# A fused attention and feed-forward kernel: the second product's seven-product form with four products in one bank, copies by ScalarE or VectorE, squares in place

## The chip, the cores and the metric

One core of one Trainium2 chip runs the whole program. Its engines are TensorE (PE, with PEld for its weight loads), VectorE (DVE), ScalarE (ACT), GpSimd (POOL) and SyncE (SP); each works through its own list of instructions in order and waits on semaphores for the others. POOL and SP also start DMA transfers. The metric is the device time of one execution in microseconds; a change is judged by the median of several runs.

## The reference

Eight batches of eight heads, 576 positions, 64 wide. Heads 0 to 3 see the last 32 positions, heads 4 to 7 every 32nd one. The attention's output, as a matrix x of 4608 tokens by 512, goes through a feed-forward layer with a squared ReLU:

```python
def _attn_ref(q, k, v):
    scores = scale * np.matmul(q, k.transpose(0, 1, 3, 2))
    scores = np.where(masks[None, :, :, :], scores, -1000000000.0)
    attn = softmax(scores)
    return np.matmul(attn, v)

def _moe_ref(x, w_in, w_out, s, b):
    h = x @ w_in                  # 4608 x 512 by 512 x 2048
    r = np.maximum(h, 0.0)
    g = s * (r * r) + b
    return g @ w_out              # 4608 x 2048 by 2048 x 512
```

Since b is one number, g @ w_out is s times (r*r) @ w_out plus b times the column sums of w_out. The kernel keeps those sums, times b, in the tile `bcs`.

## The kernel before

The attention runs over 8 batches and, in each, over 4 pairs of heads (two local pairs, two strided ones). For one pair: transposes of q and k (TensorE or DMA), scores (L656), exp on ScalarE (L674), a mask product on VectorE (L682), the product with v (L717, into banks `t` and `a`), a reciprocal (L734) and a scaling into `x_nat` (L744) on VectorE, and a transposition into `xT`. The scaling frees the bank for the next product with v.

The feed-forward layer runs over nine blocks T = 0 to 8 of 512 tokens. The first product (L1016, for T = 7 and 8 a seven-product form, L1241) gives 16 tiles h of 128 by 512; ScalarE writes relu(h) to a buffer u (L1042), and two tiles at a time are squared into `gT` by VectorE (L1052) or ScalarE (L1050). The second product takes `gT` and `w_out`: in a plain form for T = 0 and 1 (L1271), and for T = 2 to 8 in a form with seven half-size products P1 to P7 in place of eight (`ff2_seven`, L984), 16 matmuls of 256 columns each. For it, VectorE makes four sums S of parts of `gT` (L852) and once four sums of parts of `w_out` (`w_mix`, L878). The results, four quarters C11, C12, C21, C22 of a block's output, come together in PSUM and in tiles in SBUF:

- Va = s X + b from P1; then P2 goes on top of P1 in the same bank, and C11 = s X + b.
- Ua = s Y + Va from P6; Ub = Ua + (b2 - b1), the difference of the two halves of `bcs`; Vb = s Z + Ub from P7.
- C22 = s W + Vb from P5, then P3 on top of it: C12 = s W + Ub. P4 goes on top of P7: C21 = s Z + Ua.

Va, Ua, Vb (L903) and the four stores (L915) are scalar-tensor-tensor instructions of VectorE, 0.75 us each; the Ub adds (L926) are VectorE's but for one that GpSimd does.

GpSimd starts the loads of each batch (`fetch_qk`, `fetch_v`): q and k, then v, up to eighteen DMAs, behind two small copies (`gate`, L1356) that wait for the transposes of an earlier batch's k. SyncE starts the transposing DMAs and the output's.

The order of everything is fixed when the program is built. `Plan` keeps an estimate of the time of each engine; TensorE's steps come in the order of lists (attention `att`, first product `f1`, second product `f2`) as their inputs become ready by that estimate, and the work of the other engines is posted with a cost for each engine that may do it and taken up by the time it becomes ready, plus a number from the table `ORDER` for its kind and for one of four stretches of time. Where a posted job names two engines, the one that would end first gets it. PSUM has eight banks: t, a, s0, s1, f10, f11 (first product) and f20, f21 (second).

Of the kernel before, what the change touches and what calls it, by code (L numbers as in the profile page):

```python
# [1637 lines left out]
```

## Time and profile before

| | before |
|---|---|
| median of 3 runs | 297.75 us (297.03, 297.75, 298.77) |
| span of the profiled execution | 295.5 us (its own whole time is not on the page) |
| GpSimd busy | 92.8 us, 31% |
| VectorE busy | 236.8 us, 80% |
| ScalarE busy | 194.6 us, 66% |
| DMA traffic | 38.19 MB, 129 GB/s in the mean |

The page is one execution. "Busy" counts an engine's instructions, the chain follows the instruction that ended last back to what released each step, and groups put together the instructions of one source line. Starts are in us from the span's start. A row of the timeline merges instructions of one kind that follow each other: its length runs from the first start to the last end. Matmuls overlap, so their spacing is read from starts, not from lengths.

### The profile page before, as it was taken

The numbers are of one execution on the slowest core, as the hardware profiler recorded it, in microseconds if no ns is written. First come the engines' busy times: TensorE is split into PE (matmuls) and PEld (weight loads), VectorE is DVE, ScalarE is ACT, GpSimd is POOL, SyncE is SP. The second block draws the span as 40 slices with busy tenths as digits, with TensorE's granted clock in tenths as the row PEclk, the third lists the DMA queues.
The fourth block names the chain that finished last, engine by engine and source line by source line (L and its number), as shares of the span: only waits on it lengthen the run. The fifth ranks groups of instructions, "written<-read, shape, count | busy, mean of one in ns | idle before, by whom it ended". The sixth has DMA issues, their size and how long they took to land.

```text
span 295.5 us, 7106 instructions
## 1 busy us (share of the span) xinstructions
PE 289.5 (98%) x2803; PEld 219.3 (74%) x2803; DVE 236.8 (80%) x498; ACT 194.6 (66%) x334; POOL 92.8 (31%) x140
## 2 busy tenths in 40 slices
PE   7899999999999999999999999999999999999995
PEld 3775655665565567989867785779888999999984
DVE  5765977888976789768986888688899689888874
ACT  3667855897967797947873777478966564576500
POOL 8872623610961396008820195200002000000000
PEclk9999999999999999999999999999999999999999
DMA  8999999999999699979999999998430300210314
GB/s 131 180 206 203 213 184 174 208 189 128 140 160 145 98 91 161 160 138 146 162 149 147 169 168 130 134 137 213 44 104 13 109 35 2 71 38 0 109 39 143
DMA packets 106152, 38.19 MB, mean 129 GB/s; under 512 B 85414, under 2 KB 103974, under 8 KB 106118
## 3 DMA queue, kind: packets, MB, share of 16 engines
q0 software_dynamic: 60848, 18.23, 64.2%
q1 hardware_dynamic: 45270, 19.51, 36.1%
q8 instruction: 22, 0.36, 0.5%
q14 instruction: 12, 0.10, 0.1%
HBM read 36.99 MB, written 10.62 MB: 161 GB/s over the span
## 4 chain that ended last, share of the span: by engine, by line
PE 95%; POOL 3%; DVE 1%; issue 1%; ACT 0%; POOLq 0%
PE ps_f L1016 32%; PE ps_f L984 25%; PE ps_f L1271 8%; PE ps_s L656 5%; PE ps_f L1241 3%; PE ps_a L717 3%; PE ps_t L1241 2%; PE ps_s L984 2%; PE ps_a L1241 2%; PE ps_s L1241 2%; PE ps_t L717 1%; PE ps_t L984 1%; PE ps_s L1271 1%; PE ps_f L717 1%; PE ps_t L535 1%; PE ps_f L535 1%
## 5 line engine op out<-in xcount | busy, mean ns | idle before, releaser
L1016 PE MATMUL ps_f<-xT,w_in_sb 128*128 128x512 f16 (+4 forms) x568 | 115.3, 331 | 0.0
L1042 ACT ACTIVATE u<-ps_f 128x512 f16<-128x512 f32 x107 | 62.8, 595 | 34.5 <-PE ps_f L1016 32.4
L1016 PEld LDWEIGHTS <-w_in_sb 128*128 128x128 f16 x576 | 57.1, 114 | 23.1
L984 PEld LDWEIGHTS <-gT 128*128 128x128 f16 x608 | 58.3, 98 | 8.6
L984 PE MATMUL ps_f<-w_out_sb,gT 128*128 128x256 f16 x376 | 53.4, 273 | 0.0
L1271 PE MATMUL ps_f<-w_out_sb,gT 128*128 128x512 f16 x112 | 31.9, 379 | 0.0
L674 ACT ACTIVATE p_str<-ps_s 72x432 f16<-72x432 f32 (+1 forms) x45 | 21.1, 488 | 10.1 <-PE ps_s L656 9.5
L1052 DVE TENSOR_TENSOR gT<-u 128x1024 f16<-128x1024 f16 x32 | 21.8, 682 | 5.2 <-ACT u L1042 4.8
L1050 ACT ACTIVATE gT<-u 128x1024 f16<-128x1024 f16 x24 | 25.4, 1058 | 0.7
L984 PE MATMUL ps_f<-w_mix,gT 128*128 128x256 f16 x176 | 24.9, 273 | 0.0
L674 ACT ACTIVATE p_loc<-ps_s 128x384 f16<-128x384 f32 x46 | 20.7, 489 | 5.5 <-PE ps_s L656 5.1
L744 DVE TENSOR_TENSOR x_nat<-ps_a,rec 72x384 f16<-72x384 f32 (+2 forms) x45 | 23.5, 523 | 0.7
L852 DVE TENSOR_TENSOR gT<-gT 128x1024 f16<-128x1024 f16 x34 | 22.4, 683 | 0.3 <-ACT gT L1050 0.3
L415 POOL DMA_DIRECT2D v_loc<-in_v_dram x24 | 17.8, 767 | 10.1 <-DMA w_out_sb<-in_moe_w_out_dram 4.2
L984 PEld LDWEIGHTS <-S 128*128 128x128 f16 x176 | 17.1, 98 | 2.7
L717 PEld LDWEIGHTS <-p_str 72*128 72x128 f16 x256 | 13.6, 98 | 5.8 <-ACT p_str L674 0.7
L420 POOL DMA_DIRECT2D v_str<-in_v_dram x16 | 13.0, 817 | 12.8 <-PE ps_f L1016 3.7
L1271 PEld LDWEIGHTS <-gT 128*128 128x128 f16 x128 | 11.4, 98 | 6.9 <-issue 0.2
L1356 POOL COPY gate<-kT 1x1 f16<-1x1 f16 x6 | 2.2, 371 | 45.0 <-DMA kT<-ks 45.0
L984 PE MATMUL ps_f<-w_mix,S 128*128 128x256 f16 x112 | 15.0, 273 | 0.0
L734 DVE RECIPROCAL rec<-ps_a 72x6 f32<-72x6 f32 (+2 forms) x45 | 8.3, 184 | 8.4 <-PE ps_a L717 8.0
L717 PEld LDWEIGHTS <-p_loc 128*128 128x128 f16 x192 | 11.2, 98 | 5.0 <-ACT kTs L437 0.8
(235 smaller groups left out, 543.1 us busy)
## 6 DMA issues: line engine op xcount, KB each, us to landing
out_dram<-o SPq DMA_DIRECT2D x34, 256.0 KB
w_in_sb<-in_moe_w_in_dram POOLq DMA_DIRECT2D x4, 512.0 KB, 9.9
w_out_sb<-in_moe_w_out_dram POOLq DMA_DIRECT2D x4, 512.0 KB, 10.7
qs<-in_q_dram POOLq DMA_DIRECT2D x6, 288.0 KB, 8.1
ks<-in_k_dram POOLq DMA_DIRECT2D x6, 288.0 KB, 9.9
v_loc<-in_v_dram POOLq DMA_DIRECT2D x24, 72.0 KB, 9.8
ql<-in_q_dram POOLq DMA_DIRECT2D x4, 288.0 KB, 9.9
kl<-in_k_dram POOLq DMA_DIRECT2D x16, 72.0 KB, 3.7
```

Of the source, the lines that this page charges most:

```text
L415: nc.gpsimd.dma_start(out=vl[LPAD:128, h, :, 0:D], in_=v_band(b, h))
L674: nc.scalar.activation(out=st["pw", g][0:nk, 0:2 * n * nq], in_=st["s", g][0:nk, 0:2 * n * nq], func=AF.Exp, scale=scale)
L717: nc.tensor.matmul(out=st["pa", g][:, n % 6, :], lhsT=st["pw", gp_][0:nk, i * nq:i * nq + WIDE], rhs=vt[0:nk, 2 * mm + e, j, :])
L744: nc.vector.tensor_tensor(out=x_at(0, cnt), in0=st["pa", g][0:nq, 0:cnt, 0:D], in1=st["rec", g][0:nq, 0:cnt].to_broadcast([nq, cnt, D]), o ...
L852: {"V": nc.vector, "P": nc.gpsimd}[eng].tensor_tensor(out=at(out), in0=at(x), in1=at(y), op=op)
L984: nc.tensor.matmul(out=gts[name, T, t][:, 0] if halves else gts[name, T][:, t], lhsT=lhs(k, t), rhs=rhs(k), start=fresh and k == 0 and (ha ...
L1016: nc.tensor.matmul(out=gts["h", T, ft][:, lo:hi], lhsT=w_in_sb[ft // 4][:, ct].rearrange("p (x l) -> p l x", l=4)[:, ft % 4], rhs=xT[ct][: ...
L1042: nc.scalar.activation(out=u, in_=gts["h", T, ft], func=AF.Relu)
L1050: nc.scalar.activation(out=g, in_=u, func=AF.Square)
L1052: nc.vector.tensor_tensor(out=g, in0=u, in1=u, op=ALU.mult)
L1241: nc.tensor.matmul(out=st[bk][:, 256 * t:256 * t + 256], lhsT=lhs(t, c), rhs=rhs(c), start=fresh and t == c == 0, stop=t == c == 1, skip_g ...
L1271: nc.tensor.matmul(out=gts[id_], lhsT=gts[T][:, ft, ts * 128:(ts + 1) * 128], rhs=w_out_sb[:, ft, cols], start=(ft == 0), stop=(ft == NFT ...
```

## The change

It does four things.

1. For T = 2 to 7, `ff2_chain` takes the place of `ff2_seven`. P1, P6, P5 and P3 add up in one bank (A); P2 has a bank of its own (C), P7 and P4 share another (D). After P1, P6 and P5 the sum so far is kept in SBUF as s A + b: V (tile `cp_v`), U (`cp_u`) and E (again `cp_v`). Each of these three copies is either one instruction of VectorE, or a scaled copy on ScalarE followed by an add of b on GpSimd. The next product that goes into A waits for the copy alone. C11 = s C + V, C22 = s D + E, C12 = s A + b, C21 = s D + U are stored by VectorE. Block 8 keeps `ff2_seven`, with its tiles in other places.
2. relu(h) is written to `gT` and squared in place; the buffers u and their waits are gone.
3. In the seven-product form of the first product the sums go to `gT` too, and wait for the second product of block T - 2 as a whole.
4. Every number of `ORDER` is drawn anew.

Of the 18 copies, 14 go by ScalarE and GpSimd: V at T = 2, 3, 5, 6; U at T = 2 to 7; E at T = 2, 4, 6, 7. Four are VectorE's.

```diff
 ORDER = [
-    {"g": 0.0, "S": -2500.0, "in": 500.0, "w_mix": 2500.0, "wc": 0.0, "ev": 2500.0, "c21": -200.0,
+    {"g": 200.0, "S": 2500.0, "in": 500.0, "w_mix": 200.0, "wc": -200.0, "ev": 200.0,
...
+    def ff2_chain(T):
...
+        def combine(out, of, plus):
+            nc.vector.scalar_tensor_tensor(out=out, in0=gts[of, T], scalar=s_sb[:, 0:1],
+                                           in1=plus, op0=ALU.mult, op1=ALU.add)
+
+        def keep(name, half, then):
+            def add(eng):
+                nc.gpsimd.tensor_tensor(out=own_tile(name), in0=own_tile(name), in1=b[half],
+                                        op=ALU.add)
+
+            def g(eng):
+                if eng == "V":
+                    combine(own_tile(name), "A", b[half])
+                    return [d(then)]
+                nc.scalar.activation(out=own_tile(name), in_=gts["A", T], func=AF.Copy,
+                                     scale=s_sb[:, 0:1])
+                plan.post([d(then + "s")], {"P": 1700.0}, add, [d(then)])
+            return g
...
+        EV = {"V": 750.0}
+        KEEP = {"V": 750.0, "A": 700.0}
...
+            ("P1", A, "A", True, cut(0, 0), w(0, 0), gn(0), [("bcs",)],
+             [([d("P1")] + ([("c11", T - 1)] if T > SEVEN else []), KEEP,
+               keep("V", 0, "Va"), [d("Vas")])]),
+            ("P2", C, "C", True, cut(0, 1), w(1, 0), gn(1), [],
+             [([d("P2"), d("Va")], EV, store(0, 0, "C", lambda: own_tile("V")),
+               [d("c00"), C])]),
+            ("P6", A, "A", False, tile_of("S2") if roomy(T) else cut(0, 0), mix(2), sn(2),
+             [("w_mix", 2), d("Vas")],
+             [([d("P6")] + prior, KEEP, keep("U", 0, "Ua"), [d("Uas")])]),
+            ("P7", Dd, "D", True, tile_of("S"), mix(3), sn(3), [("w_mix", 3)], []),
+            ("P5", A, "A", False, cut(1, 0), mix(1), sn(1), [("w_mix", 1), d("Uas")],
+             [([d("P5"), d("c00")], KEEP, keep("V", 1, "Ea"), [d("Eas")]),
+              ([d("P7"), d("Ea")], EV, store(1, 1, "D", lambda: own_tile("V")), [d("c11")])]),
+            ("P3", A, "A", False, tile_of("S4") if roomy(T) else cut(0, 1), w(1, 1), sn(4),
+             [d("Eas")], [([d("P3")], EV, store(0, 1, "A", lambda: b[1]), [A])]),
+            ("P4", Dd, "D", False, cut(1, 1), mix(4), gn(1), [("w_mix", 4), d("c11")],
+             [([d("P4"), d("Ua")], EV, store(1, 0, "D", lambda: own_tile("U")), [d("c10"), Dd])]),
...
             def rl(eng):
-                if at % 2 == 0:
-                    gts["u", T, pair] = up.tile([128, 2, PS], FP16, tag="u", name="u")
-                u = gts["u", T, pair][:, at % 2]
+                u = gts[T][:, ft]
...
-                    nc.scalar.activation(out=g, in_=u, func=AF.Square)
+                    nc.scalar.activation(out=g, in_=g, func=AF.Square)
                 else:
-                    nc.vector.tensor_tensor(out=g, in0=u, in1=u, op=ALU.mult)
...
+                    nc.vector.tensor_tensor(out=g, in0=g, in1=g, op=ALU.mult)
+
+            s.posts = [([key], {"A": 600, **({"V": 690} if T == 0 else {})}, rl, [("u", T, ft), group])]
...
-            far = ff_order(T - 1)[8 + 4 * u:12 + 4 * u] if u < 2 else [
-                x + y for x in (ft - 4, ft + 4) for y in (0, 1)]
-            free = [("g", T - 1 if u < 2 else T, x) for x in far]
+            free = [("F2", T - 2)]
```

**GpSimd at the loads of batch 6.** Before, its list there goes from the loads of one batch to the gates of the next, with nothing that another engine's arithmetic waits for:

```order
L415 DMA v_loc0_101<-in_v_dram 96x6x64 x4
L420 DMA v_str0_103<-in_v_dram 72x8x64 x4
L1356 COPY gate_164<-kT2_2571 1x1 x2
L387 DMA ql_2679<-in_q_dram 96x6x64 x4
L387 DMA kl_2684<-in_k_dram 96x6x64 x4
```

After, with lines of the changed kernel (L906 is the add of b; the first two rows are T = 2's U and E, the next V and U of T = 3):

```order
L906 TENSOR_TENSOR cp_u_114<-cp_u_114,bcs_91 128x512
L906 TENSOR_TENSOR cp_v_113<-cp_v_113,bcs_91 128x512
L1448 COPY gate_160<-kT2_2068 1x1 x2
L390 DMA ql_2189<-in_q_dram 96x6x64 x4
L390 DMA kl_2194<-in_k_dram 96x6x64 x4
L408 DMA qs_1364<-in_q_dram 72x4x512
L408 DMA ks0_115<-in_k_dram 72x4x512
L418 DMA v_loc0_95<-in_v_dram 96x6x64 x4
L423 DMA v_str0_97<-in_v_dram 72x8x64 x4
L906 TENSOR_TENSOR cp_v_113<-cp_v_113,bcs_91 128x512
L906 TENSOR_TENSOR cp_u_114<-cp_u_114,bcs_91 128x512
L1448 COPY gate_160<-kT2_2526 1x1 x2
```

T = 2's E add now stands ahead of the gates for batch 6, and T = 3's V add behind that batch's last load.

**VectorE at the last pair of batch 5.** Before, the scalings that free banks t and a follow each other, with a square between:

```order
L734 RECIPROCAL rec_2476<-ps_t0_156 72x6
L744 TENSOR_TENSOR x_nat_2461<-ps_t0_156,rec_2476 72x384
L734 RECIPROCAL rec_2491<-ps_a0_159 72x6
L1052 TENSOR_TENSOR gT_2384<-u_2472 128x1024
L744 TENSOR_TENSOR x_nat_2461<-ps_a0_159,rec_2491 72x384
```

After, T = 3's store of C11 (L901), which reads `cp_v`, stands between that pair's first reciprocal and its scaling:

```order
L737 RECIPROCAL rec_2452<-ps_t0_152 72x6
L901 SCALAR_TENSOR_TENSOR o_2455<-ps_f21_159,sb_all_85,cp_v_113 128x512
L747 TENSOR_TENSOR x_nat_2440<-ps_t0_152,rec_2452 72x384
L737 RECIPROCAL rec_2474<-ps_a0_155 72x6
L855 TENSOR_TENSOR gT_1890<-gT_1890 128x4x256
```

What frees bank t for the next product with v is now behind an instruction that reads GpSimd's result.

**VectorE at T = 7's C22.** Before, the sums of the first product (ISA, each frees a bank that TensorE wants next) and T = 7's stores stand like this:

```order
L1161 ISA u_4102<-ps_a0_159,U_4062 128x2x256
L1184 TENSOR_TENSOR gT_3974<-u_4102 128x1024
L1161 ISA u_4183<-ps_t0_156,E_4174 128x2x256
L915 SCALAR_TENSOR_TENSOR o_4196<-ps_s1_158,sb_all_91,Ua_4030 128x512
L1161 ISA u_4183<-ps_t0_156,U_4142 128x2x256
```

After, the store of C22 (the first L901) follows the second sum; between the first sum and the second stands a square (L1278), whose two operands lie in SBUF. GpSimd's add to E runs at the same time, since its copy comes from P5, whose matmuls end just before:

```order
L1258 ISA gT_3850<-ps_t0_152,U_3974 128x2x256
L1278 TENSOR_TENSOR gT_3850<-gT_3850 128x1024
L1258 ISA gT_3850<-ps_a0_155,E_4075 128x2x256
L901 SCALAR_TENSOR_TENSOR o_4096<-ps_s0_153,sb_all_85,cp_v_113 128x512
L1258 ISA gT_3850<-ps_a0_155,U_4049 128x2x256
L901 SCALAR_TENSOR_TENSOR o_4113<-ps_s1_154,sb_all_85,bcs_91 128x512
```

The store of C22 came here before at another place, from Vb, with no add of GpSimd ahead of it.

More of the change, by code (lines that the diff above doesn't have):

```diff
@@ L87, in flush @@
             self.free[eng] = end
-            p[2](eng)
-            for k in p[3]:
+            more = p[2](eng)
+            for k in list(p[3]) + (more if isinstance(more, list) else []):
                 if isinstance(k, Group):
@@ L308, in lay_out @@
     p_taken = {True: 0, False: 0}
+    cp_v = const.tile([128, 512], FP32, name="cp_v")
+    cp_u = const.tile([128, 512], FP32, name="cp_u")
+    own_db = kT_loc[1][:, 0:512].bitcast(FP32)[:, None, :]
     SR = 80
@@ L880, in mix_post, with own_tile @@
             before = [("w_mix", i)]
-        plan.post([("ev", SEVEN - 1, ts) for ts in range(4)], {"V": 350.0},
-                  lambda eng: nc.vector.tensor_tensor(
-                      out=bcs[:, 256:512], in0=bcs[:, 256:512], in1=bcs[:, 0:256],
-                      op=ALU.subtract), [("dbc",)])
+    def own_tile(name):
+        at = {"V": cp_v, "U": cp_u, "Ub": qD_str[0].rearrange("p t e c -> p (t e c)")}[name]
+        return (at if name != "Ub" else at[:, 0:1024].bitcast(FP32)).rearrange(
+            "p (t m) -> p t m", t=2)
@@ new lines, in lay_out, with d, store, g @@
+    CHAIN = {NBLK - 2: ("f2", F2B, "s", SB)}
+    def ff2_chain(T):
+        A, C, Dd = [Group(*CHAIN.get(T, ("f2", F2B))) for _ in range(3)]
+        b = [bcs[:, None, 256 * i:256 * i + 256].to_broadcast([128, 2, 256]) for i in range(2)]
+        def d(x):
+            return (x, T)
+        def combine(out, of, plus):
[13 more added lines that the diff above has]
+            return g
+        def store(i, k, of, plus):
+            def g(eng):
+                o = op.tile([128, 2, 256], FP32, tag="o", name="o")
+                combine(o, of, plus())
+                r0 = T * PS + 256 * i
+                nc.sync.dma_start(
+                    out=out[r0:r0 + 256, 256 * k:256 * k + 256].rearrange(
+                        "(t p) m -> p t m", p=128), in_=o)
+            return g
+        EV = {"V": 750.0}
+        KEEP = {"V": 750.0, "A": 700.0}
+        def cut(i, j):
+            return lambda k, t: part_of(T, i, j)[:, k, 128 * t:128 * t + 128]
+        def tile_of(w):
+            return lambda k, t: gts[w, T][:, k, 128 * t:128 * t + 128]
+        def w(j, c):
+            return lambda k: w_out_sb[:, H * j + k, 256 * c:256 * c + 256]
+        def mix(i):
+            return lambda k: w_mix[i][:, k]
+        def gn(j):
+            return lambda k: [("g", T, H * j + k)]
+        def sn(i):
+            return lambda k: [("S", T, i, k // 4)]
+        prior = [("c10", T - 1)] if T > SEVEN else []
+        seq = [
+            ("P1", A, "A", True, cut(0, 0), w(0, 0), gn(0), [("bcs",)],
[15 more added lines that the diff above has]
+             [([d("P4"), d("Ua")], EV, store(1, 0, "D", lambda: own_tile("U")), [d("c10"), Dd])]),
+        ]
+        steps = []
+        for key, group, name, fresh, lhs, rhs, needs, more, posts in seq:
+            for t in range(2):
+                for k in range(H):
+                    def f(k=k, t=t, group=group, name=name, fresh=fresh, lhs=lhs, rhs=rhs):
+                        if fresh and t == k == 0:
+                            gts[name, T] = bank(group).rearrange("p (t m) -> p t m", t=2)
+                        nc.tensor.matmul(out=gts[name, T][:, t], lhsT=lhs(k, t), rhs=rhs(k),
+                                         start=fresh and t == k == 0,
+                                         stop=t == 1 and k == H - 1, skip_group_check=True)
+                    s = Step(f, 110, needs=needs(k) + more,
+                             group=group if fresh and k == t == 0 else None)
+                    if t == 1 and k == H - 1:
+                        s.keys = [d(key)] + ([("F2", T)] if key == "P4" else [])
+                        s.posts = posts
+                    s.pos = T + 0.25 + (len(steps) + 1) / 112.0
+                    steps.append(s)
+        return steps
@@ L886, in ff2_seven @@
     def ff2_seven(T):
         last = T == NBLK - 1
-        banks = {NBLK - 1: (("t", TB), ("a", AB), ("f1", F1B), ("f1", F1B)),
-                 NBLK - 2: (("f2", F2B), ("f2", F2B), ("s", SB), ("s", SB))}
-        X, W, Y, Z = [Group(*x) for x in banks.get(T, [("f2", F2B)] * 4)]
+        db = own_db.to_broadcast([128, 2, 256])
+        plan.post([("bcs",)] + [("s", (B - 1, m), 2) for m in range(2)], {"V": 350.0},
+                  lambda eng: nc.vector.tensor_tensor(
+                      out=own_db[:, 0], in0=bcs[:, 256:512], in1=bcs[:, 0:256],
+                      op=ALU.subtract), [("dbc",)])
@@ L892, in ff2_seven @@
+        X, W, Y, Z = [Group(*x) for x in (("t", TB), ("a", AB), ("f1", F1B), ("f1", F1B))]
         Ws = [W, Group("f2", F2B)]
         b1 = bcs[:, None, 0:256].to_broadcast([128, 2, 256])
-        db = bcs[:, None, 256:512].to_broadcast([128, 2, 256])
         def d(x):
@@ L1151, in keep, with u_at @@
                 return g
[L1153 to L1157 removed]
+            def u_at(row, j, T=T, ft=ft):
+                if T not in gts:
+                    gts[T] = gp.tile([128, NFT, PS], FP16, tag="gT", name="gT")
+                return gts[T][:, ft + 8 * row:ft + 8 * row + 2, 256 * j:256 * j + 256]
             def add(row, j, of, name, st=st, u_at=u_at):
@@ L1173, in relu, with square @@
                         "p (t x) -> p t x", t=2))
-            def square(row, st=st, T=T, ft=ft):
+            def square(row, T=T, ft=ft):
                 def g(eng):
-                    if T not in gts:
-                        gts[T] = gp.tile([128, NFT, PS], FP16, tag="gT", name="gT")
-                    x = st["u", row]
                     g_ = gts[T][:, ft + 8 * row:ft + 8 * row + 2, :]
                     if eng == "A":
-                        nc.scalar.activation(out=g_, in_=x, func=AF.Square)
+                        nc.scalar.activation(out=g_, in_=g_, func=AF.Square)
                     else:
-                        nc.vector.tensor_tensor(out=g_, in0=x, in1=x, op=ALU.mult)
+                        nc.vector.tensor_tensor(out=g_, in0=g_, in1=g_, op=ALU.mult)
                 return g
```

26 lines of the change are left out of this document (7 added, 19 removed), and 77 rows, old and new, of the table ORDER.

## The prediction

> **What bounds the kernel now.** I read the page's first parts, then the table of stretches, then what TensorE waited for, then the timeline of each engine at the places that the change touches.
>
> ```profile
> span 295.5 us, 7106 instructions
> PE 289.5 (98%) x2803; PEld 219.3 (74%) x2803; DVE 236.8 (80%) x498; ACT 194.6 (66%) x334; POOL 92.8 (31%) x140
> PE 95%; POOL 3%; DVE 1%; issue 1%; ACT 0%; POOLq 0%
> ```
>
> TensorE is busy for 289.5 of 295.5 us and makes 95% of the chain that ends last. Busy alone would not prove that it runs at its pace, so the stretches and the spacing of the matmuls come next (columns: stretch, length, then busy us and count of PE, PEld, DVE, ACT and POOL, clock, DMA share, GB/s).
>
> ```profile
> 0.00:15.00 15.00, 12.21 (x155) 7.89 (x156) 10.23 (x36) 6.86 (x12) 12.26 (x23) 1.00 1.11 156
> 100.00:150.00 50.00, 50.00 (x507) 39.65 (x506) 41.23 (x90) 38.26 (x66) 27.30 (x40) 1.00 1.23 138
> 250.00:292.00 42.00, 42.00 (x388) 39.09 (x386) 34.78 (x54) 17.85 (x24) 0.00 (x0) 1.00 0.17 58
> 292.00:295.50 3.50, 0.36 (x4) 0.08 (x1) 0.49 (x2) 0.00 (x0) 0.00 (x0) 1.00 0.43 150
> PE ps_t L527 <- DMA ql<-in_q_dram: 0.9, 1, 0.9
> PE ps_s L1521 <- PEq L1622: 0.8, 1, 0.8
> PE ps_f L717 <- DVE v_loc L437: 0.7, 1, 0.7
> PE ps_f L717 <- POOL v_loc L437: 0.4, 1, 0.4
> ```
>
> ```profile
> 152.16 0.29 PE L717 MATMUL ps_t<-v_str,p_str 72*128 72x65 f16 x4
> 152.29 1.03 PE L1016 MATMUL ps_f<-xT,w_in_sb 128*128 128x512 f16 x4
> 153.15 0.82 PE L984 MATMUL ps_f<-w_out_sb,gT 128*128 128x256 f16 x6
> 153.81 0.38 PE L1016 MATMUL ps_f<-xT,w_in_sb 128*128 128x512 f16 x1
> 205.47 0.23 PE L656 MATMUL ps_s<-qD_str,kT 128*72 128x144 f16 x1
> 205.62 0.35 PE L717 MATMUL ps_a<-v_loc,p_loc 128*128 128x65 f16 x6
> ```
>
> TensorE's listed waits are four, 2.8 us, all in the first 15 us; the granted clock is 1.00 throughout. Four matmuls of 512 columns start within 0.86 us (0.215 each), six of 256 within 0.66 (0.110 each): those are their spacings everywhere. From 50 us on I found one start (205.47 to 205.62) over 0.06 us later than its kind's. So the middle holds **almost nothing to win**, 0.2 us; up to 1.2 if every small excess went.
>
> **The change, part by part.** TensorE's list is as long after as before, with the same matmuls of the same sizes, and the first 40 us of it are the same row by row; so are the last 112 matmuls and the evictions behind them. Head (with its 2.8 us of waits) and tail (the 3.5 us from 292.0) stay. What can differ is only whether TensorE waits in between.
>
> ```profile
> L915 DVE SCALAR_TENSOR_TENSOR o<-ps_f,sb_all,Vb 128x512 f32<-128x512 f32 x6 | 4.5, 747 | 0.1
> L926 DVE TENSOR_TENSOR Ub<-Ua,bcs 128x512 f32<-128x512 f32 x6 | 4.2, 692 | 0.2
> L437 ACT COPY E<-ps_f 128x512 f32<-128x512 f32 x2 | 1.2, 587 | 4.6 <-PE ps_f L1241 4.6
> L852 DVE TENSOR_TENSOR gT<-gT 128x1024 f16<-128x1024 f16 x34 | 22.4, 683 | 0.3 <-ACT gT L1050 0.3
> L1052 DVE TENSOR_TENSOR gT<-u 128x1024 f16<-128x1024 f16 x32 | 21.8, 682 | 5.2 <-ACT u L1042 4.8
> ```
>
> *Removed and moved work.* VectorE loses 14 scalar-tensor-tensors (58 to 44) and 6 Ub adds: 14 x 0.747 + 6 x 0.692 = 14.6 us. ScalarE gains 14 copies, 14 x 0.587 = 8.2 us. GpSimd gains 14 adds and loses one. I cost the relief and the copies at nothing: no wait of TensorE on either engine is left after 15 us, and both have room (DVE 41 of 50 us, ACT 38 of 50). Squares in place cost nothing: writing over its own input took 683 ns, from another tile 682. If this cover failed, one late copy would cost at most its 0.59 us.
>
> *Term 1: the T=3 add behind the loads of batch 6.* In the changed order the add of b to T=3's V stands on GpSimd directly behind the two gates and eighteen loads for batch 6. Times of these, before (the start, the length, the row):
>
> ```profile
> 134.39 0.33 POOL L1356 COPY gate<-kT 1x1 f16<-1x1 f16 x1 [1.12 <-DMA kT<-ks]
> 141.46 0.79 POOL L405 DMA_DIRECT2D ks<-in_k_dram  x1
> 150.86 0.81 POOL L420 DMA_DIRECT2D v_str<-in_v_dram  x1 [2.11 <-PE ps_t L717]
> 108.70 0.75 POOL L405 DMA_DIRECT2D ks<-in_k_dram  x1
> 116.35 0.80 POOL L420 DMA_DIRECT2D v_str<-in_v_dram  x1 [1.50 <-PE ps_s L656]
> 176.09 0.77 POOL L405 DMA_DIRECT2D ks<-in_k_dram  x1
> 187.39 0.80 POOL L420 DMA_DIRECT2D v_str<-in_v_dram  x1 [0.63 <-DMA ks<-in_k_dram]
> 78.82 0.72 POOL L405 DMA_DIRECT2D ks<-in_k_dram  x1
> 89.06 0.80 POOL L420 DMA_DIRECT2D v_str<-in_v_dram  x1 [2.32 <-DMA ks<-in_k_dram]
> 221.54 1.65 POOL L926 TENSOR_TENSOR Ub<-Ua,bcs 128x512 f32<-128x512 f32 x1 [33.35 <-DVE Ua L903]
> ```
>
> The last load starts when that of ks, eight loads earlier, has landed: 9.40 us after it here, 7.65, 11.30 and 10.24 in the blocks of batches 5, 7 and 4. The gates wait for transposes on SyncE that stand in the same row as before, so I keep 134.4, plus 0.2 us for T=2's add, which now stands ahead of them. The block then ends at 151.67 + 0.2 = 151.9 and the add at 153.5. VectorE meets the store of C11 (which reads this V) much earlier:
>
> ```profile
> 150.06 0.35 PE L717 MATMUL ps_t<-v_str,p_str 72*128 72x65 f16 x6
> 150.75 0.18 DVE L734 RECIPROCAL rec<-ps_t 72x6 f32<-72x6 f32 x1
> 150.97 0.55 DVE L744 TENSOR_TENSOR x_nat<-ps_t,rec 72x384 f16<-72x384 f32 x1
> ```
>
> These are batch 5's last head pair. Its reciprocal starts 0.69 us after its six matmuls; in the changed order those six stand at 150.8, so VectorE is at the store at about 151.5 and stops for 2.0 us. Behind the store stands that pair's x_nat, which frees bank t; TensorE's next four matmuls want t. They stood at 152.16; in the changed order 35 more matmuls of 256 columns and 11 fewer of 512 are ahead of them: 152.16 + 35 x 0.109 - 11 x 0.216 = 153.6. VectorE ends the store at 153.5 + 0.75 and x_nat 0.45 later, 154.7. TensorE waits **1.1 us**. Bounds: 7.65 in place of 9.40 gives nothing, 11.30 gives 3.0.
>
> *Term 2: VectorE held while GpSimd adds.*
>
> ```profile
> 221.38 0.67 DVE L1099 TENSOR_TENSOR ks<-ks,w_in_sb 128x1024 f16<-128x1024 f16 x1
> 222.60 1.14 DVE L852 TENSOR_TENSOR S<-gT 128x1024 f16<-128x1024 f16 x1 [0.55 <-PE ps_f L984]
> 223.66 1.28 DVE L1099 TENSOR_TENSOR v_str<-w_in_sb,ks 128x1024 f16<-128x1024 f16 x2
> ```
>
> The only add of before ran from 221.54 to 223.19. The one tensor-tensor that VectorE started within it (two operands in SBUF) took 1.14 us in place of 0.683, and ended 0.55 after the add: it was held. I let each such operation wait for the add's end. Four third copies (E) go by ScalarE and GpSimd, at T=2, 4, 6, 7, and their store follows soon. The walk for T=7, with E's copy at 274.95 by the count of matmuls: copy to 275.55, add to 277.25; the square, due at 276.0, waits until then; 0.60 later the sum that frees bank a starts and ends at 278.5, where TensorE wants it at 277.65: 0.9 us, and 0.1 more for the C22 store behind. The same walk gives 0.4 at T=6, and nothing at T=2, whose store has 0.6 us to spare, and at T=4, where it comes out even: **1.4 us**. Bounds: 0 if nothing is held; 1.65 for each of these four adds, 6.6, if all of each falls on TensorE.
>
> A rule weighed: the Trainium skill, "SBUF — State Buffer", section "Who interferes with whom", says that a VectorE instruction with two SBUF inputs and a GpSimd one that reads SBUF exclude each other, and that whichever issued first keeps the port to its end. The held operation agrees (1.14 for 0.683). By that rule the add of 221.54 would itself have waited for the one that ran until 222.05, and an add alone would be 0.5 us shorter than the row; the sum would be the rival's below.
>
> *Sum:* 1.1 + 1.4 - 0.2 = +2.3 us on a span of 295.5. The page gives no time of its execution beyond the span; the median of the three runs, 297.75, is 2.2 above it, and I keep that: 297.8. With it, **300.0 us**.
>
> **The rivals.**
> - *A shorter add.* If 221.54 to 222.05 was waiting (VectorE ran a two-operand instruction just then), an add alone is 1.14 us. Term 1 falls to 0.6, T=7 to 0.5, T=6 to 0: +0.9, **298.7 us**. For it: the overlap in the rows. Against: GpSimd's spans are rough, and under VectorE's load adds would wait again.
> - *Not slower: the loads end early.* If ks lands within 7.7 us of its issue, as for batch 5, the add is done by 151.8 and term 1 is nothing; and if the held squares find TensorE 0.7 us ahead in VectorE's results, so is term 2. **297.6 us.** It decides at a last load of batch 6 that starts before 149.2. Against it: three of the four blocks took longer (9.40, 11.30, 10.24).
> - *Faster.* All small excess goes, none comes: -1.2, **296.5 us**. The ceiling by the rows above.
> - *Much slower.* The other ten adds hold masks and sums too, 0.25 us of TensorE each (half of the 0.46 that the row was lengthened by): +2.5 more, **302.5 us**.
>
> **How the numbers follow.** About 0.5% (1.5 us) is what a measurement of this kernel can tell from no change. Forecast 0.42 (alone 299.0 to 301.6), shorter add 0.18, loads early 0.22, faster 0.04, much slower 0.14. Slower by over 1.5 us: 0.38 + 0.03 + 0.14 = 0.55. Same: 0.04 + 0.15 + 0.21 + 0.02 = 0.42. Faster: 0.03. The range leaves out the fast end and half of the much slower case: 297.0 to 302.2.
>
> **What would show it.** Right: TensorE's waits gain rows behind 15 us; a gap before `ps_t` at about 153.6 ended by VectorE, VectorE's store there idle on GpSimd, and that add starting at the end of batch 6's loads; tensor-tensors of over 1 us where GpSimd adds. Wrong: busy TensorE of 50.00 in each stretch of 50 us as before; the T=3 add ended before 151.5; adds of GpSimd over VectorE's tensor-tensors at 0.68.

## The result

The changed kernel takes 300.31 us in its profiled execution, on a span of 298.5 us. Against the kernel before (297.47 us, median of five) the ratio is 1.0106, 95% interval 1.0067 to 1.0144. A second measurement, of the same kernel beside eleven executions of before, gave 1.0149 (1.0122 to 1.0176). So it is slower by 1 to 1.5%, and it also scatters: in the second measurement five executions took 300.4 to 303.2 us, the eleven of before beside them 297.07 to 297.66. Three more of its executions, 305.34, 307.19 and 305.93 us at mean clocks of 0.989 to 0.992, count as slow and are left out of these ratios, though a long pause of TensorE gave such clocks by itself below (late_add, dummy), so the loss may be larger. The forecast was 300.0.

The page after, its first parts (span; busy time of each engine; the chain that ended last):

```profile
span 298.5 us, 7091 instructions
PE 290.7 (97%) x2803; PEld 219.3 (73%) x2803; DVE 236.6 (79%) x492; ACT 191.3 (64%) x335; POOL 109.7 (37%) x153
PE 90%; POOL 4%; DVE 2%; issue 2%; ACT 1%; POOLq 0%; DVEq 0%
```

TensorE's share of the chain fell from 95% to 90%. VectorE is as busy as before (236.8 then) although it does 20 instructions of the second product less: nine squares came back to it from ScalarE (37 and 8 at their two lines, 32 and 4 before), and its instructions beside GpSimd's adds are longer. What TensorE waited for, in us (the rows of the first 15 us are left out):

```profile
PE ps_t L720 <- DVE x_nat L747: 0.7, 1, 0.7
...
PE ps_a L1333 <- DVE gT L1258: 0.3, 1, 0.3
```

The first is the place that the prediction named. Its timeline (start, length; in brackets how long the engine had been idle and what ended that):

```profile
151.34 0.82 POOL L423 DMA_DIRECT2D v_str<-in_v_dram  x1 [0.65 <-PE ps_f L1120]
152.17 1.28 POOL L906 TENSOR_TENSOR cp_v<-cp_v,bcs 128x512 f32<-128x512 f32 x1
151.46 0.19 DVE L737 RECIPROCAL rec<-ps_t 72x6 f32<-72x6 f32 x1 [0.17 <-PE ps_t L720]
153.49 0.75 DVE L901 SCALAR_TENSOR_TENSOR o<-ps_f,sb_all,cp_v 128x512 f32<-128x512 f32 x1 [1.83 <-POOL cp_v L906]
154.15 0.55 DVE L747 TENSOR_TENSOR x_nat<-ps_t,rec 72x384 f16<-72x384 f32 x1
153.62 0.38 PE L1120 MATMUL ps_f<-xT,w_in_sb 128*128 128x512 f16 x1
154.75 0.28 PE L720 MATMUL ps_t<-v_str,p_str 72*128 72x65 f16 x4 [0.75 <-DVE x_nat L747]
```

ScalarE had copied this V by 147.07; the add of b waited 5.1 us for its turn behind batch 6's loads. VectorE stood still for 1.83 us, bank t came free at 154.70, and TensorE's next matmul started 1.13 us after the last, where its kind takes 0.216: 0.91 us late. The second, at T=7:

```profile
276.95 1.27 POOL L906 TENSOR_TENSOR cp_v<-cp_v,bcs 128x512 f32<-128x512 f32 x1 [5.65 <-ACT cp_v L913]
277.34 1.43 DVE L1278 TENSOR_TENSOR gT<-gT 128x1024 f16<-128x1024 f16 x1
278.69 0.68 DVE L1258 CUSTOM_DVE_ANT_0 gT<-ps_a,E 128x512 f16<-128x512 f32 x1
279.42 0.60 PE L1333 MATMUL ps_a<-p_loc,w_in_sb 128*128 128x256 f16 x4 [0.27 <-DVE gT L1258]
```

The square, 0.69 us elsewhere, took 1.43 and ended 0.55 after the add. To count all of it, I use one measure from here on: **late starts**, the sum over the matmuls from 50 us on that start over 15 ns later than their kind's usual spacing (matmuls that a lower clock spaces out count too). Before it is 0.15 us, after 2.00: 0.91 at 154, 0.62 around 279, 0.23 at 255 (T=6), 0.22 at 82. The last matmul ends at 294.21 against 292.36, 1.85 later. That leaves 1.14 of the 2.99 us of span, and it lies behind the last matmul: 4.32 us there against 3.18. The DMA queues in that last stretch, before first, then after (packets, MB, share of 16 engines):

```profile
q1 hardware_dynamic: 554, 0.52, 47.7%
```

```profile
q1 hardware_dynamic: 554, 0.52, 35.8%
q14 instruction: 2, 0.02, 1.8%
```

The same 554 packets of the last stores; but two transfers on the queue of the program's own code now lie among them. They are 8 KB each, start 0.93 and 1.13 us after the last matmul and take 0.47 and 0.79 us. The last packets of the stores ended at 2.95 us in place of 1.91.

### The profile page after: what moved, and what is told of

It is laid out like the page before. It is cut to its first block, busy times and chain, and to the rows that moved or that the text cites. A ratio compares the mean times of both kernels' runs of the same rounds, so it can differ in the third digit from the quotient of the medians.

```text
span 298.5 us, 7091 instructions
## 1 busy us (share of the span) xinstructions
PE 290.7 (97%) x2803; PEld 219.3 (73%) x2803; DVE 236.6 (79%) x492; ACT 191.3 (64%) x335; POOL 109.7 (37%) x153
## 4 chain that ended last, share of the span: by engine, by line
PE 90%; POOL 4%; DVE 2%; issue 2%; ACT 1%; POOLq 0%; DVEq 0%
PE ps_f L1120 32%; PE ps_f L976 20%; PE ps_f L1363 7%; PE ps_s L659 5%; PE ps_s L976 3%; PE ps_a L720 3%; PE ps_f L1333 2%; PE ps_f L1088 2%; PE ps_a L1333 2%; PE ps_s L1333 2%; PE ps_t L1333 1%; PE ps_t L720 1%; PE ps_t L1088 1%; PE ps_s L1363 1%; PE ps_f L720 1%
## 5 line engine op out<-in xcount | busy, mean ns | idle before, releaser
L1144 ACT ACTIVATE gT<-ps_f 128x512 f16<-128x512 f32 x107 | 63.5, 596 | 36.0 <-PE ps_f L1120 35.1
L976 PEld LDWEIGHTS <-gT 128*128 128x128 f16 x544 | 51.7, 98 | 9.5 <-issue 0.2
L976 PE MATMUL ps_f<-w_out_sb,gT 128*128 128x256 f16 x336 | 48.5, 273 | 0.0
L1153 DVE TENSOR_TENSOR gT<-gT 128x1024 f16<-128x1024 f16 x37 | 26.4, 715 | 10.7 <-ACT gT L1144 10.2
L906 POOL TENSOR_TENSOR cp_v<-cp_v,bcs 128x512 f32<-128x512 f32 x8 | 10.7, 1335 | 44.5 <-ACT cp_v L913 44.4
L855 DVE TENSOR_TENSOR gT<-gT 128x1024 f16<-128x1024 f16 x34 | 25.0, 743 | 0.1
L747 DVE TENSOR_TENSOR x_nat<-ps_a,rec 96x384 f16<-96x384 f32 (+2 forms) x45 | 23.4, 519 | 0.5
L906 POOL TENSOR_TENSOR cp_u<-cp_u,bcs 128x512 f32<-128x512 f32 x6 | 7.6, 1271 | 39.5 <-ACT cp_u L913 39.5
L1151 ACT ACTIVATE gT<-gT 128x1024 f16<-128x1024 f16 x19 | 20.1, 1058 | 0.5
L1363 PEld LDWEIGHTS <-gT 128*128 128x128 f16 x128 | 11.3, 98 | 6.8 <-ACT gT L1151 0.5
L855 DVE TENSOR_TENSOR S<-gT 128x1024 f16<-128x1024 f16 x18 | 13.6, 753 | 2.8 <-PE ps_f L976 2.6
L737 DVE RECIPROCAL rec<-ps_a 96x6 f32<-96x6 f32 (+2 forms) x45 | 8.3, 184 | 8.2 <-PE ps_a L720 7.8
```

The costliest lines, as they stand in the source:

```text
L747: nc.vector.tensor_tensor(out=x_at(0, cnt), in0=st["pa", g][0:nq, 0:cnt, 0:D], in1=st["rec", g][0:nq, 0:cnt].to_broadcast([nq, cnt, D]), o ...
L855: {"V": nc.vector, "P": nc.gpsimd}[eng].tensor_tensor(out=at(out), in0=at(x), in1=at(y), op=op)
L906: nc.gpsimd.tensor_tensor(out=own_tile(name), in0=own_tile(name), in1=b[half], op=ALU.add)
L976: nc.tensor.matmul(out=gts[name, T][:, t], lhsT=lhs(k, t), rhs=rhs(k), start=fresh and t == k == 0, stop=t == 1 and k == H - 1, skip_group ...
L1144: nc.scalar.activation(out=u, in_=gts["h", T, ft], func=AF.Relu)
L1151: nc.scalar.activation(out=g, in_=g, func=AF.Square)
```

## The experiments

In all of them TensorE's list of matmuls is that of the changed kernel, but for the one with the old priorities. "Last" is the end of the last matmul, "end" the time from there to the end of the span, both in the first execution of each, the one with a trace.

| run | ratio to before (95%) | last | late starts | end |
|---|---|---|---|---|
| before | 1 | 292.36 | 0.15 | 3.18 |
| after | 1.0106 (1.0067 to 1.0144) | 294.21 | 2.00 | 4.32 |
| again | 1.0149 (1.0122 to 1.0176) | 294.79 | 2.69 | 4.01 |
| no_add | 1.0055 (1.0034 to 1.0076) | 294.20 | 1.17 | 3.65 |
| v_all | 1.0046 (1.0033 to 1.0059) | 293.04 | 0.96 | 3.51 |
| t3_v | 1.0092 (1.0079 to 1.0105) | 294.56 | 2.35 | 3.87 |
| late_add | 1.0356 (1.0336 to 1.0377) | 302.56 | 10.56 | 3.89 |
| dummy | one execution, 309.73 us | 303.93 | 11.94 | 4.02 |
| shift | 1.0145 (1.009 to 1.0199) | 294.54 | 2.42 | 3.50 |
| fix | 1.0017 (1.0001 to 1.0034) | 292.78 | 0.67 | 3.48 |
| fix2 | 1.0373 (1.0337 to 1.041) | 304.78 | 12.45 | 3.19 |
| old_order | 1.0374 (1.034 to 1.0409) | 301.45 | 9.48 | 3.54 |
| fix3 | 1.003 (1.0018 to 1.0042) | 293.22 | 1.19 | 3.59 |

### The changed kernel again (again)

No edit.

> The changed kernel itself, once more, to see which part of its +3.0 us of span comes back. In the first profile the last matmul ended 1.85 us later than before (294.21 against 292.36), and from there to the end of the span it took 4.3 us against 3.1. Theory (two new waits, and a last store that landed late by chance): the last matmul ends at 294.0 to 294.4 again, with the waits of 0.9 us at about 153.6 and 0.4 us at about 278.9; the stretch behind it is 3.0 to 4.4 us, not always 4.3. Rival (the stretch behind is longer because of the change): it is 4.1 to 4.5 us here and in every kernel with the same order.

The wait at 154 was 1.59 us here, not 0.9: batch 6's last load started at 151.91, 9.07 us after the load of ks, and the add at 152.74. The waits at 255 and 279 came back to within 0.01 us. The last matmul, at 294.79, is outside the 294.0 to 294.4 that I gave. The end was 4.01, within the theory's 3.0 to 4.4 and just under the rival's 4.1 to 4.5; what makes it longer is settled further down (shift).

### Without GpSimd's adds (no_add)

```diff
             def add(eng):
-                nc.gpsimd.tensor_tensor(out=own_tile(name), in0=own_tile(name), in1=b[half],
-                                        op=ALU.add)
+                return
```

> Without the 14 adds of GpSimd (b is left out of the V, U and E that ScalarE copies, so the results of blocks 1 to 7 lack it there); TensorE's list is the same. Theory (both new waits come from these adds): the waits at 153.6 (0.91 us), 255.1 (0.23 us) and 278.9 to 279.9 (0.55 us) go, 1.7 us, and the last matmul ends at 292.5; the 0.2 us at 82.0, ahead of the first add, stays. Every square and sum of VectorE in blocks 1 to 7 takes 0.65 to 0.70 us. Rival (the new order alone makes TensorE wait): the last matmul ends at 294.2 as with the adds.

The waits at 154, 255 and 279 are gone but for 0.07 us at 277, as the theory says. Yet the last matmul ends at 294.20, the number of the rival. Two things make up for what was won: the first 50 us took 0.79 us longer in this execution, most of it a wait of 0.7 us for a load of q that neither side had, and there is a new wait of 0.85 us at 203, which the next run but one shows too. The second has no add in it and comes from the new order alone, so there the rival has a point.

### Sums by VectorE alone (v_all)

```diff
-                nc.scalar.activation(out=own_tile(name), in_=gts["A", T], func=AF.Copy,
-                                     scale=s_sb[:, 0:1])
+                combine(own_tile(name), "A", b[half])
```

and no add, as above.

> VectorE scales and adds b in one instruction, as before the change, in the places where ScalarE copied and GpSimd added; TensorE's list is the same. Theory: the waits go as without the adds, and VectorE, 236.6 + 14 x 0.75 = 247 us busy, has the room: the last matmul ends at 292.5 to 292.9. Rival (VectorE has no room, which is what the copies on ScalarE buy): new waits of TensorE on VectorE, 0.3 to 0.7 us at several of the 14 places, and the last matmul ends at 294 to 297.

The last matmul ends at 293.04, 0.14 over the theory's range. Two places show that VectorE has less room: 0.28 us at 147.8, 0.29 at 245.2, both below the 0.3 to 0.7 of the rival. Its four executions lie within 0.8 us (298.33 to 299.11).

### Only block 3's V by VectorE (t3_v)

```diff
+                if (T, then) == (3, "Va"): combine(own_tile(name), "A", b[half])
+                else: nc.scalar.activation(out=own_tile(name), in_=gts["A", T], func=AF.Copy, scale=s_sb[:, 0:1])
```

and no add for that one.

> Only block 3's V is made by VectorE (in one instruction, where ScalarE's copy stood); the 13 other adds stay. Theory (the 0.91 us at 153.6 comes from the add that stands behind the loads of batch 6): that wait goes, VectorE's store at 151.7 starts without a stop of 1.8 us, the rest stays: the last matmul ends at 293.3. Rival (VectorE is late there anyway, being busy without a pause from 144.5 to 151): TensorE still waits 0.4 to 0.9 us at 153.6 and the last matmul ends at 293.7 to 294.2.

The wait at 154 is gone; VectorE's store starts at 151.84 without a stop. 0.28 us came at 147.9, where VectorE's longer instruction stands. But the time was given back at 202.7, so the last matmul ends at 294.56 and not at the 293.3 of the theory; this wait is a third weak place of the new order. VectorE and TensorE there, in this run:

```profile
201.27 0.62 DVE L440 COPY qD_str<-qT 64x576 f16<-64x576 f16 x2 [2.37 <-DMA qT<-qs]
201.93 0.76 DVE L685 TENSOR_TENSOR p_loc<-p_loc,masks 128x1152 f16<-128x1152 f16 x1
202.74 0.37 PE L720 MATMUL ps_a<-v_loc,p_loc 128*128 128x65 f16 x6 [0.80 <-DVE p_loc L685]
```

and VectorE in the kernel before:

```profile
200.91 0.76 DVE L682 TENSOR_TENSOR p_loc<-p_loc,masks 128x1152 f16<-128x1152 f16 x1 [0.22 <-ACT p_loc L674]
202.74 0.75 DVE L915 SCALAR_TENSOR_TENSOR o<-ps_f,sb_all,Ub 128x512 f32<-128x512 f32 x1 [1.07 <-PE ps_t L717]
203.41 0.61 DVE L437 COPY qD_str<-qT 64x576 f16<-64x576 f16 x2
```

Before, VectorE spread batch 7's query tile (its copies from qT into qD_str) behind the mask product that TensorE needs; in the new order these copies stand ahead of it, VectorE comes to them some 4 us earlier, and it is stopped by the transposing DMA. In the first profile of the changed kernel it was stopped too, for 1.24 us, but TensorE came late enough (202.42) for that to cost nothing: the 0.9 us lost at 154 covered it.

### Three adds more ahead of block 3's V (late_add)

```diff
+                for _ in range(3 if (T, then) == (3, "Va") else 0): nc.gpsimd.tensor_tensor(out=idle_t, in0=b[0], in1=b[1], op=ALU.add)
```

> Three more adds of GpSimd, into a tile that nothing reads, directly ahead of its add for block 3's V: that add ends 3 x 1.28 = 3.8 us later. Theory (TensorE's wait at about 154 is the end of this add, one for one): the wait is 0.9 to 1.6 + 3.8 = 4.7 to 5.4 us and the last matmul ends at 298.0 to 298.6. The second question is why runs of the changed kernel lie at a mean clock of 0.994 to 0.997 (303.2 and 302.5 us), and the 11 of before beside them at 0.998 to 1.0. If a long pause of TensorE lowers its clock, the clock falls here to 0.99 to 0.995 in nearly every run, the matmuls of 512 columns behind the pause start over 0.25 us apart, and the span is 2 to 4 us longer than the pause alone makes it: 304 to 307. Rival (the clock has nothing to do with the pause): 0.999, a span of 302 to 303.

The wait is 5.89 us, the add ends at 158.22. From the first profile (0.91 us with an add that ended at 153.45) 4.77 us of delay became 4.98 of waiting: one for one, within 0.2. The clock then falls. This execution's stretches behind the pause (stretch, length, busy us and count of PE, PEld, DVE, ACT, POOL; the clock, the DMA share, GB/s):

```profile
154.00:158.00 4.00, 0.00 (x0) 0.00 (x0) 0.00 (x0) 0.13 (x1) 3.84 (x4) 1.00 1.67 105
158.00:162.00 4.00, 2.48 (x12) 1.39 (x12) 3.35 (x8) 0.74 (x2) 0.22 (x1) 0.58 1.56 162
162.00:166.00 4.00, 4.00 (x17) 2.16 (x15) 0.69 (x1) 1.14 (x2) 1.27 (x1) 0.57 0.65 123
166.00:170.00 4.00, 4.00 (x28) 2.77 (x27) 1.77 (x3) 1.31 (x3) 0.18 (x1) 1.00 0.75 153
```

Until 165.5 the matmuls of 512 columns start 0.427 us apart in place of 0.216. That alone costs 2.9 us on top of the pause; all four executions had a mean clock under 0.99. A further 0.69 us of late starts, here and in the next run, lies at 205, where TensorE waits for a store of VectorE; VectorE had been slowed beside GpSimd's work from 201 on, one square taking 1.09 us in place of 0.68, and two copies beside GpSimd's own 1.48 in place of 0.61.

### A second, useless add behind E of blocks 6 and 7 (dummy)

```diff
+                if T >= 6 and then == "Ea": nc.gpsimd.tensor_tensor(out=idle_t, in0=b[0], in1=b[1], op=ALU.add)
```

> A second add of GpSimd, into a tile that nothing reads, directly behind its adds for E of blocks 6 and 7. Theory (VectorE's square there is held by the adds themselves, whoever needs their result): the square that started at 277.3 and took 1.43 us is held until the second add has ended, about 2.7 us, the wait of TensorE for ps_a grows from 0.43 to 1.7 us, and the one at 255.1 from 0.23 to 0.5 or more; the last matmul ends 1.3 to 2.6 us later than without. If VectorE gets the port between the two adds, the square takes 1.4 us as before, the second add takes over 1.8 us, and TensorE's wait stays under 0.6. Rival (VectorE and TensorE wait for the result of the add, not for a shared port): nothing reads the second add, so both waits stay at 0.43 and 0.23 us, with a square of 1.43 us and a second add of 1.28.

GpSimd and VectorE at T=6:

```profile
260.96 1.27 POOL L906 TENSOR_TENSOR cp_v<-cp_v,bcs 128x512 f32<-128x512 f32 x1 [5.69 <-ACT cp_v L913]
262.19 1.72 POOL L907 TENSOR_TENSOR idle_t<-bcs 128x512 f32<-128x512 f32 x1
261.18 1.59 DVE L855 TENSOR_TENSOR S<-gT,S 128x1024 f16<-128x1024 f16 x1
262.70 1.76 DVE L1278 TENSOR_TENSOR gT<-gT 128x1024 f16<-128x1024 f16 x1
```

The sum of VectorE ended 0.54 after the first add. Nothing reads the second one, and still the square beside it took 1.76 us and ended 0.55 after it; TensorE's wait there rose from 0.23 to 1.31 us. So it is the overlap that holds VectorE, not a result. At T=7 the square got through between the two adds (1.43 us as before), the second add took 1.72, and TensorE's wait stayed at 0.43: the two engines take turns, and who waits goes next.

The run had a surprise ahead of its edit, at T=3, where it is the changed kernel itself. GpSimd's timeline there:

```profile
144.15 0.72 POOL L408 DMA_DIRECT2D ks<-in_k_dram  x1 [1.59 <-DMA ql<-in_q_dram]
...
156.70 0.81 POOL L423 DMA_DIRECT2D v_str<-in_v_dram  x1 [5.24 <-DMA ks<-in_k_dram]
157.53 1.27 POOL L906 TENSOR_TENSOR cp_v<-cp_v,bcs 128x512 f32<-128x512 f32 x1
```

The last load started 12.55 us after that of ks, TensorE waited 6.48 us, and the clock fell as in the run before, which cost another 2.6 us. So the changed kernel can meet a pause of this length by itself.

### More instructions for VectorE (shift)

```diff
-                combine(o, of, plus())
+                combine(o, of, plus()); nc.vector.memset(idle_t[0:1, 0, 0:1], 0.0)
```

> The changed kernel with one write of a single element by VectorE ahead of each store's DMA (24 more instructions, spread over blocks 1 to 7), which brings VectorE's list back to the length at which the fetch of its last code came at 281 to 283 us. Theory (the end is longer because two fetches of code, 8 KB each, fall among the packets of the last stores, one of them for VectorE): one fetch is left there, and from the last matmul to the end of the span it takes 3.4 to 3.7 us, in place of 4.0 to 4.3; the waits of TensorE ahead of it stay (0.9 to 1.6 us at 154, 0.4 at 279), within 0.3 us for the added instructions. Rival (the longer end has another cause): it stays at 3.9 to 4.4 us.

The end took 3.50 us and holds one fetch; VectorE's came 12.8 us before the last matmul. The queues from the last matmul on (columns as before):

```profile
q1 hardware_dynamic: 554, 0.52, 43.7%
q14 instruction: 1, 0.01, 0.7%
```

The waits ahead are those of the changed kernel (1.32 us at 155), and so is the scatter: 299.81 to 301.77 us in three executions, 303.97 in a fourth at a clock of 0.994.

### Four things mended (fix)

V of block 3 and E of blocks 6 and 7 by VectorE (as in t3_v), the single-element writes of shift, and

```diff
-                copy_on(eng, out=st["q"][hs, :, e, :], in_=st["qT"][hs, :, 0:nq])
+                copy_on("P" if b == 7 else eng, out=st["q"][hs, :, e, :], in_=st["qT"][hs, :, 0:nq])
```

This moved three spreads of batch 7 from VectorE to GpSimd: the strided one that the expectation names, and the two local ones.

> Four things together: V of block 3 and E of blocks 6 and 7 made by VectorE in one instruction; the spread of batch 7's last query tile by GpSimd, so that VectorE isn't stopped by its transpose; the 24 single-element writes of the run beside it. Theory (the loss is these places and nothing else): the waits at 154, 203, 255 and 279 go, 0.3 us at 147.8 and 0.2 at 82 are left, the last matmul ends at 292.7 to 293.2, the end behind it takes 3.4 to 3.7 us, span 296.1 to 296.9, time 297.9 to 298.7: within 0.5% of before, over by 0.6 to 1.4 us, and the same in each run. Rival (the loss moves to the next places as fast as one is mended): the last matmul ends at 293.8 or later.

All as the theory said: last matmul at 292.78, end 3.48, span 296.3, and nine executions between 297.97 and 298.53 us. The waits at 154, 203, 255 and 279 and the second fetch in the end were the loss, taken together, since this run doesn't part the four; most of the scatter went with them.

### The add ahead of the last loads, and SyncE's fetch (fix2)

As fix, but V of block 3 by ScalarE and GpSimd with batch 6's four `v_str` loads behind its add, and eight small copies of SyncE's:

```diff
-            nc.gpsimd.dma_start(
+            (late_vs.append if b == 6 else lambda f: f())(lambda h=h: nc.gpsimd.dma_start(
                 out=vs[:, h, :, 0:D],
-                in_=v[b, 4 + h].rearrange("(p j) d -> p j d", j=ST))
+                in_=v[b, 4 + h].rearrange("(p j) d -> p j d", j=ST)))
...
+                [f() for f in late_vs if (T, then) == (3, "Va")]
...
+                [nc.sync.dma_start(out=idle_t[0:1, 1, 0:64], in_=bcs[0:1, 0:64]) for _ in range(2 * (T in (1, 2)))]
```

> As the run with four things mended, with two differences. Block 3's V is again copied by ScalarE and added to by GpSimd, but the add stands ahead of batch 6's last four loads (v_str) instead of behind them; and SyncE gets eight small copies of its own early on, so that its last fetch of code too comes before the last stores. Theory (the place in GpSimd's queue made the wait at 154, not the use of GpSimd): the add ends at about 149, VectorE's store at 151.5 doesn't stop for it, the 0.28 us at 147.8 (VectorE's longer instruction there) goes as well, and the last matmul ends at 292.4 to 292.7. The end behind it takes 3.1 to 3.3 us without any fetch in it. Span 295.5 to 296.0, time 297.3 to 297.8, that of before. Rival (the loads are moved into a wait of their own): the wait at 154 goes, batch 6's v_str comes late, and TensorE waits 0.5 us or more between 175 and 190.

The small copies spoilt it: they kept SyncE's transposes waiting, GpSimd's loads for batch 6 began at 143.40 in place of 136, and TensorE waited 2.2, 4.6, 2.0 and 1.5 us at places between 156 and 215 where fix doesn't wait. The theory's time of 297.3 to 297.8 was missed by 9 us or more, and the run says nothing of the add's place. It does answer for the end: no fetch is left in it, and it took 3.19 us, before's 3.18. It also brackets the clock: it stayed at 1.00 behind the pause of 2.2 us and fell behind that of 4.6. Two of its stretches, behind the one pause and behind the other (columns as above, the clock third from the end):

```profile
156.00:158.00 2.00, 1.75 (x16) 1.26 (x16) 2.00 (x7) 0.79 (x2) 1.26 (x2) 1.00 1.93 170
...
174.00:176.00 2.00, 0.31 (x3) 0.06 (x2) 0.89 (x3) 1.52 (x3) 0.00 (x0) 0.50 0.77 165
```

### The priorities of before (old_order)

The changed kernel with the table `ORDER` of before, its first numbers for instance:

```diff
-    {"g": 200.0, "S": 2500.0, "in": 500.0, "w_mix": 200.0, "wc": -200.0, "ev": 200.0,
+    {"g": 0.0, "S": -2500.0, "in": 500.0, "w_mix": 2500.0, "wc": 0.0, "ev": 2500.0, "c21": -200.0,
```

> The changed kernel with the priorities of before: the same matmuls, the squares in place and the four gathered products, but only ten adds of GpSimd, and the one that meets batch 7's loads stands in front of its last eight. Theory (the losses are places where the order put something close behind a load or beside an add, and the priorities choose the places): the waits are elsewhere and of other sizes; without a priority fitted to this kernel I expect more of them, 2 to 8 us of TensorE in all, 299 to 305. Rival (the new priorities are what costs): the last matmul ends at 292.4 to 293.0 and the time is 297.5 to 298.5.

More than I expected: 9.48 us of late starts (1.6 of it from a lower clock), at other places, and 306.9 to 309.7 us. The largest, 3.1 us at 178, is in good part the add behind loads once more: GpSimd adds b to block 3's E behind the first ten loads of batch 7, and VectorE's store of C22, which TensorE waits for, stops 1.40 us for it:

```profile
176.16 1.29 POOL L906 TENSOR_TENSOR cp_v<-cp_v,bcs 128x512 f32<-128x512 f32 x1
177.49 0.75 DVE L901 SCALAR_TENSOR_TENSOR o<-ps_f,sb_all,cp_v 128x512 f32<-128x512 f32 x1 [1.40 <-POOL cp_v L906]
```

Behind this pause, which follows some smaller waits, the clock fell too; that tightens the bracket to 2.2 to 3.1 us (columns as above):

```profile
174.00:178.00 4.00, 1.07 (x18) 0.81 (x17) 2.60 (x3) 1.32 (x4) 4.00 (x5) 1.00 1.52 147
178.00:180.00 2.00, 1.71 (x9) 1.18 (x9) 1.98 (x6) 0.00 (x0) 2.00 (x4) 0.55 1.52 82
```

So the old priorities are no remedy: with them the same code has three and a half to nearly five times the late starts (2.00 and 2.69 in the changed kernel's two traces). The new ones have weak places of their own, at 82, 154 and 203.

### The add ahead of the last loads alone (fix3)

Against fix2:

```diff
-                [nc.sync.dma_start(out=idle_t[0:1, 1, 0:64], in_=bcs[0:1, 0:64]) for _ in range(2 * (T in (1, 2)))]
```

> The run before without SyncE's eight small copies, which had kept its transposes waiting (batch 6's loads began at 143.4 us in place of 135 to 136). So against the run with four things mended one thing differs: block 3's V is copied by ScalarE and its b added by GpSimd, ahead of batch 6's last four loads instead of behind them. Theory (the wait at 154 was the add's place in GpSimd's queue): loads begin at 135 to 136, the add ends at 149 to 150, TensorE doesn't wait at 147.8 nor at 154, the last matmul ends at 292.4 to 292.7, one fetch of code is left in the end behind it (3.5 us), span 295.9 to 296.2, time 297.6 to 298.0. Rival (an add of GpSimd costs there wherever it stands, since it then delays the loads): a wait of 0.3 us or more at 147 to 155, or a new one of 0.5 us or more between 175 and 190.

Both sides were partly right, and the last matmul, at 293.22, came later than the theory's 292.4 to 292.7. In this execution the last load started late again, 12.67 us after that of ks (at 144.98). GpSimd's timeline:

```profile
148.66 1.75 POOL L906 TENSOR_TENSOR cp_v<-cp_v,bcs 128x512 f32<-128x512 f32 x1
...
157.65 0.82 POOL L423 DMA_DIRECT2D v_str<-in_v_dram  x1 [4.81 <-DMA ks<-in_k_dram]
```

What cost 6.5 us and the clock in dummy cost nothing, since the add was done by 150.4; twelve executions lie between 297.85 and 299.21. But here the add ran beside VectorE's sums, two of which took 1.65 and 1.22 us in place of 0.65, and TensorE was late by 0.60 us at 150 to 151.5. So the queue's place makes the large, uncertain wait, and an add beside busy VectorE a small one. No version beats the kernel before.

## Why the prediction was right or wrong

*What bounds it.* Right: with TensorE busy to 98% there was nothing to win, and nothing was won by VectorE's relief. ScalarE's copies took 0.68 to 0.69 us in place of the 0.587 that I read from another copy, which cost nothing. The ceiling of 0.2 us held; the 0.09 at 205.6 went.

*Term 1, the add behind the loads.* Right in mechanism, and in the profiled execution nearly to the tenth: end of the block 151.9 forecast and 152.16 found, end of the add 153.5 and 153.45, bank t free at 154.7 and 154.70, wait 1.1 and 0.91. Part of that was luck. Two parts of it were off and made up for each other: the load of ks started at 143.78, some 2 us later than I had it, and the last load 7.56 us after that in place of 9.40. The first came in about equal parts from a block that began later (136.03; 134.97 before) and from a wait that I left out: the load of ks itself waits for a load of ql, eight loads earlier, to land (1.19 us here, 1.59 in dummy, none before the change). Wrong was the bound of 3.0 us. I took it from the longest of four blocks of loads (11.30 us); three more traces with the add in this place, unedited there, gave waits of 1.3, 1.6 and, at 12.55 us behind a load of ks that itself started at 144.15, 6.5, and behind the last the clock fell, a price that no row of before could show. Most of the scatter goes with this add: in t3_v, where it alone is gone, four executions lie within 0.7 us, and beside them five of the changed kernel within 2.8 (again); in fix nine lie within 0.6, beside four of shift within 4.2. In fix3, with the add ahead of the last loads, twelve lie within 1.4. That the execution at a mean clock of 0.994 (303.2 us) met a pause of over 2.2 us is argued, since it has no trace; one at 0.997 (302.5 us) shows nothing, as an execution of fix at 0.997 took 298.36. The Trainium skill, "TensorE: Matmul & The Clock Gate", part 1, gives half the clock after an idle window of about 3.4 us; the spacing of 0.427 for 0.216 agrees with the half, and here a pause of 3.1 us, somewhat shorter than that window, was enough (old_order), one of 2.2 us not (fix2).

*Term 2, VectorE held.* The mechanism was shown by dummy; its size was off. I forecast 1.0 us at T=7 and 0.4 at T=6, and 0.62 and 0.23 came: 0.85 for 1.4. The mis-sized term is the add, 1.65 us by the only row of before; alone it takes 1.26 to 1.29 (twelve of the fourteen; the other two 1.46 and 1.58). The row of 1.65 held waiting for VectorE, as the rival "a shorter add" said, though its 1.14 was too short. With 1.28 for 1.65 my walk gives 0.63 at T=7, where 0.62 came, and 0.03 at T=6, where 0.23 came; there the held instruction was a sum (1.59 us), not the square, and why the walk is 0.2 short stays open. The other eleven adds cost TensorE nothing in this trace, so "much slower" didn't come by its own mechanism.

*Head and tail stay.* Half wrong. The last matmuls and evictions were indeed the same, to 0.01 us. What I didn't look at is the code's own transfers: 1.14 of the 2.99 us lie behind the last matmul, and the end shrinks from 4.32 to 3.50 us with one fetch taken out of it (shift) and to 3.19 with both (fix2).

*Not in the prediction at all.* The spread of batch 7's query tile ahead of the mask product: I compared the order where adds stand, not where a copy had moved past a DMA. It cost 0 in the profiled execution and in v_all, where the transposing DMA landed earliest (199.3), and 0.85 to 0.97 in two others.

*The sum.* +2.3 was forecast and +3.0 measured in the profiled execution: 0.91 + 0.85 + 0.22 at 82 (in every kernel with the new order; its cause wasn't tested), less the 0.15 of before, 1.85 with rounding, and 1.14 behind the last matmul. The number came out near by luck: two terms were too large by 0.7 together, and 1.14 and 0.22 were missed. It fits an execution whose loads land early, too; in the second trace the first term alone was 1.59.

## What to carry to other kernels

Look for any result that a busy engine waits for behind a queue of DMA issues: its time is that of the slowest load on a bad execution, not of the profile at hand, and a kernel with such a place scatters. When one such wait goes, look at once for the next step that had hidden behind it. When instructions are taken out of an engine's list, see where its last fetches of code come to lie, above all if the end is a store.
